# Causal masks as GpSimd selections, a division over two PSUM banks, more transposes by DMA, and chained weight loads in a one-core transformer block

## The chip, the cores and the metric

The kernel runs on one core of a Trainium2 chip. The core has five engines that run side by side, each with its own queue of instructions in order: PE (matrix products; PEld is its weight load), DVE (the vector engine), ACT (the scalar engine), POOL (GpSimd) and SP, which here issues every DMA. Engines wait for each other by semaphores. The metric is the device time of one execution in microseconds (us), smaller being better. The span of a profile runs from the first to the last instruction.

## What is computed

The reference is one transformer block over 2048 tokens of width 640, conditioned by a vector c: sliding-window attention with 32 heads of width 20, then a gated MLP of width 1536. Cut to what matters here:

```python
mod = (silu(c) @ w_mod).reshape(1, 6, 1, 640)         # sa, ca, ga, sb, cb, gb
h = layernorm(x) * (1 + ca) + sa
q, k, v = heads(h @ wqkv)                             # 32 heads, Dh = 20
scores = q @ k.T * 20 ** -0.5
mask = (i - j >= 0) & (i - j < 256)                   # i: query, j: key
p = softmax(where(mask, scores, -1e9))
x = x + ga * ((p @ v) @ wo)
h = layernorm(x) * (1 + cb) + sb
x = x + gb * ((sigmoid(h @ w_gate) * (h @ w_up)) @ w_down)
```

A query sees its own key and the 255 before it. The mask is therefore a triangle at the two ends of the window and all ones between them. The kernel applies it after the exponential, by making the forbidden weights zero.

## The kernel before

The 2048 tokens are cut into 8 chunks of 256 (numbered 0 to 7). For each chunk `ln1` loads x, takes mean and variance on DVE (L627, L629), the power -0.5 on POOL (L632, L634), normalizes (L637) and turns the result so that features lie on partitions (`hT`). For the first `NPT = 3` chunks PE turns it by products with an identity (`pe_transposes`, evicted at L670 or L671); for the others a DMA transposes it (L643) and `modulate` (L651, L652) applies scale and shift. `qkv` makes Q and K in a staging tile `stg`, head by head padded to 32 columns, and turns them into `QT` and `KT`: for the first `NPT` chunks again by identity products (evicted at L696 or L697), for the others by DMA. V stays as it comes.

`attention` works on 16 heads at a time (q = 0, 1). A **set** is a PSUM tile S of 128 x 4 x 512 scores: two groups of keys lie on its partitions 0 to 63 and 64 to 127 (called its halves), four heads in its four banks, and blocks of 64 query columns side by side. `plan` says which block stands where. Chunk 0 has four sets of 6 blocks for each q; the other chunks have five sets of 8 blocks, four of the kind "1" and one that gathers what remains, the kind "2". ACT takes the exponential of a whole set into one of 8 buffers E (L795). Then the masks: each is a TENSOR_TENSOR multiply of E by a mask tile made at the start, on DVE or POOL, as the planner chooses. The kinds are "c" (chunk 0, two of 128 x 4 x 128 a set), "d" (128 x 4 x 64) and "f" (128 x 4 x 128) on a set of kind "1" (L809), and "2" (all 2048 columns, L802) on a set of kind "2".

When the sets of a q are done, a **burst** of 128 small products (64 in chunk 0) multiplies E by V into two PSUM tiles of the pool M, in two phases of which the second waits for the first. V carries a column of ones, so the softmax's denominator comes out beside each head. `norm` then works on each of the two banks by itself: DVE transposes 32 x 32 blocks (L865), takes reciprocals (L866), multiplies (L868) and transposes back (L872). DMAs write the result to DRAM and read it back turned, `outproj` multiplies by wo and adds x (L908), the second layer norm follows, a DMA transposes, and `mlp` does gate, up and down for the chunk (L932 tanh, L934 product, L946 residual).

Nothing of this order is written out by hand. Every operation is recorded with a list of engines that may do it, a cost for each of these, a priority and what it reads and writes; score sets also have a due time (`PACE0 + PACE` times their number). A list scheduler, `Prog.schedule`, then places one operation after another on the engine where it can start first by these costs. The order on each engine is fixed when the program is built; at run time an engine takes its instructions in that order and waits where it must. SP is such an engine too: a DMA that has to wait holds back all that stand behind it. A changed cost can therefore move any instruction. `Prog.emit` adds the semaphores.

The weights (w_mod in three parts, wqkv, wo, w_gate, w_up, w_down) are loaded by 33 DMAs in the first 46 us. The second and third part of w_mod lie for a while where w_up and four of the E buffers will be, and the first where w_down will be. POOL multiplies wo and w_down by the gates ga and gb (L972 and L982).

Of the kernel before, what the change touches and what calls it, by code (L numbers as in the profile page):

```python
# [8 lines left out]
ALU = mybir.AluOpType  # L9
# [42 lines left out]
class Tile:  # L52
    __slots__ = ("pool", "name", "res", "slot", "ops", "left", "rel", "prev")

    def __init__(self, pool, name):
        self.pool = pool
        self.name = name
        self.res = {}
        self.slot = None
        self.ops = []  # L60
        self.left = 0
        self.rel = []
        self.prev = []

# [10 lines left out]
class Op:  # L75
    __slots__ = ("engs", "eng", "fn", "dur", "lat", "deps", "succ", "tiles", "prio", "seq", "nleft", "ready", "start",
                 "end", "mode", "fence", "key", "val", "signal", "work", "tmin", "isdma", "tag", "done")


class Prog:  # L80
# [8 lines left out]
    def op(self, eng, fn, dur, reads=(), writes=(), prio=50.0, lat=0.05, work=None, tmin=0.0, extra=(), tag="", hold=(),  # L89
           mode=0, fence=None):  # L90
        o = Op()
        o.mode = mode
        o.fence = fence
        o.engs = eng if isinstance(eng, tuple) else (eng,)
# [51 lines left out]
    def schedule(self):  # L146
# [27 lines left out]
        def slots_for(o):  # L174
# [4 lines left out]
            for t in o.tiles:  # L179
                if t.slot is None:  # L180
# [100 lines left out]
    def emit(self):  # L281
# [6 lines left out]
        for e in ENGS:  # L288
            for o in self.order[e]:
# [13 lines left out]
                need[o] = ws  # L303
        for e in ENGS:
# [55 lines left out]
def c_pool(n):  # L360
    return 0.22 + n / 460.0
# [7 lines left out]
NPT = 3  # L369
# [6 lines left out]
def build(nc, A_x, A_wqkv, A_wo, B_x, B_w_gate, B_w_up, B_w_down, c, w_mod, out, S=2048):  # L376
# [20 lines left out]
    mk_c = sb("mk_c", [128, 128])  # L397
    mk = sb("mk", [128, 320])
    mk_d, mk_f, mk_2 = mk[:, 0:64], mk[:, 64:192], mk[:, 192:320]
# [19 lines left out]
    p_T1 = sbpool("T1", 2, [128, 512], F32)  # L419
    p_Tn = sbpool("Tn", 2, [128, 512])  # L420
    p_On = sbpool("On", 2, [128, 1024])
    p_Dr = sbpool("Dr", 2, [128, 16], F32)
# [6 lines left out]
    p_M = Pool("M", [nc.alloc_psum_tensor(f"M{i}", [128, 512], F32) for i in range(4)])  # L429
# [9 lines left out]
    R_mA, R_shB, R_scB, R_gbc, R_mh, R_mk = R("mA"), R("shB"), R("scB"), R("gbc"), R("mh"), R("mk")  # L439

    def dma(dst, src, work, reads=(), writes=(), prio=50.0, tmin=0.0, tag="dma", extra=(), nonc=False, hold=()):
# [5 lines left out]
        return A("sp", fn, 0.43, reads=reads, writes=writes, prio=prio, work=work, tmin=tmin, tag=tag, extra=extra, hold=hold)  # L447

# [19 lines left out]
    for i in range(len(p_Tn.aps)):  # L468
        p_Tn.init[i].append(A("pool", lambda e, g, i=i: e.memset(p_Tn.aps[i][:], 0.0), 0.6, writes=[R("ti")], prio=3))

    mk_u = p_sig.aps[1][:].bitcast(BF16)[:, 0:320]

    def mk_ini(e, g):
        e.memset(mk_c[:], 1.0)
        e.memset(mk[:], 1.0)
        return e.memset(mk_u, 1.0)
    A("pool", mk_ini, 0.8, writes=[R_mk], prio=2)

    def keep(ap, w, base, cm):
        A("pool", lambda e, g: e.affine_select(ap, ap, pattern=[[-cm, w]], compare_op=ALU.is_ge, fill=0.0, base=base,  # L480
                                               channel_multiplier=cm), 0.35, reads=[R_mk], writes=[R_mk], prio=2)
    keep(mk_c[:], 128, 0, -1)
    for u in (0, 3):
        keep(mk[:, 64 * u:64 * u + 64], 64, 0, -1)
    for u in (1, 2):
        keep(mk[:, 64 * u:64 * u + 64], 64, -1, 1)
    for u in (0, 2):
        keep(mk_u[:, 64 * u:64 * u + 64], 64, 64, -1)
    for u in (1, 4):
        keep(mk_u[:, 64 * u:64 * u + 64], 64, -65, 1)  # L490
    p_sig.init[1].append(A("dve", lambda e, g: e.tensor_copy(mk[64:128, :], mk_u[64:128, :]), 0.3, reads=[R_mk], writes=[R_mk], prio=2))
# [13 lines left out]
    def load_wm(i, kt, prio, tmin=0.0):  # L505
        return dma(lambda: wm_ap[i][:, kt, :], lambda: wm_src[:, kt, i * 1280:(i + 1) * 1280], 0.86, writes=[Rm[i][kt]],
                   prio=prio, tmin=tmin, tag=f"wm{i}")
# [4 lines left out]
    def load_w3(k, prio):  # L512
        i = ("wq", "wk", "wv").index(k)
        dma(lambda: W3[k][:], lambda: wqkv_src[:, :, i * D:(i + 1) * D], 2.2, writes=[R_w3[k]], prio=prio, tag=k)
# [11 lines left out]
    dma(lambda: wo[:], lambda: A_wo.rearrange("(t p) f -> p t f", p=128), 2.2, writes=[R_wo], prio=0.5, tag="wo")  # L526
# [508 lines left out]
```

The softmax here doesn't subtract the row's maximum and nothing guards it: scores larger than these inputs give would overflow.

## Time and profile before

The times of 13 runs lie between 367.14 and 376.35 us, with a median of 371.05 us.

| | before |
|---|---|
| time of the profiled execution | 370.57 us |
| its span | 368.4 us |
| mean granted PE clock | 0.977 |
| PE busy | 337.9 us (92% of the span) |
| DVE busy | 260.9 us (71%) |
| ACT busy | 219.2 us (59%) |
| POOL busy | 139.9 us (38%) |
| masks on POOL (L802, L809) | 73 instructions, 95.8 us |
| masks on DVE (L802, L809) | 69 instructions, 41.8 us |
| products of scores and of bursts (L555) | 1920 and 1920 |
| DMA | 37.61 MB |

The span is 2.2 us shorter than the execution's time: what lies around it. A group of instructions in the profile carries its line, engine, operation, the tiles it writes and reads, its shape, its total busy time, the mean time of one, and the idle time of its engine just before it with what ended that. Products of PE overlap, so that the busy time of PE is more than the sum of its useful cycles; what counts for this kernel is when it is not busy, and when its clock is granted at half.

### The profile page before, as it was taken

What the parts mean: (1) busy time and instruction counts of PE and PEld (TensorE: products, weight loads), DVE (VectorE), ACT (ScalarE), POOL (GpSimd) and SP (SyncE); (2) the same over time, 40 slices, a digit from 0 to 9 for tenths busy, and PEclk for the clock granted to TensorE, in tenths of its full rate; (3) what the DMA queues carried; (4) which work ended last, traced back from release to release, by engine and by line L of the source; (5) the groups of instructions that cost most, each with busy time, mean ns of one, the idle gap of its engine ahead of it and who ended that gap; (6) DMA issues with size and microseconds to landing.
All of it is one profiled execution on the core that took longest, in us unless ns stands there. A gap on an engine that the chain in (4) does not pass through costs nothing.

```text
span 368.4 us, 13956 instructions
## 1 busy us (share of the span) xinstructions
PE 337.9 (92%) x6088; PEld 244.5 (66%) x6088; DVE 260.9 (71%) x543; ACT 219.2 (59%) x237; POOL 139.9 (38%) x160
## 2 busy tenths in 40 slices
PE   6898866989899899999999989899899999999996
PEld 2665433656566576667675667677767868888784
DVE  5369997999769996865857699678668866432232
ACT  1395783777688877888687667566676711122120
POOL 6127695682454632452354526255232300100000
PEclk9899995999899999999999999999999999999999
DMA  6999932206742736293015411131041122010101
GB/s 201 382 396 392 372 93 63 72 4 115 144 112 63 153 79 123 61 146 94 21 45 97 106 41 31 44 107 35 5 112 39 34 74 76 20 55 1 37 1 37
DMA packets 65181, 37.61 MB, mean 102 GB/s; under 512 B 41440, under 2 KB 61920, under 8 KB 65120
## 3 DMA queue, kind: packets, MB, share of 16 engines
q1 hardware_dynamic: 65120, 36.72, 36.7%
q8 instruction: 48, 0.79, 0.9%
q14 instruction: 13, 0.11, 0.1%
HBM read 21.96 MB, written 5.24 MB: 74 GB/s over the span
## 4 chain that ended last, share of the span: by engine, by line
PE 67%; DVE 8%; issue 3%; ACT 2%; POOL 0%; DVEq 0%; ACTq 0%
PE M L554 56%; PE M L555 6%; PE S L555 5%; DVE T L865 1%; DVE x L637 1%; ACT E L795 1%; DVE st L627 1%; DVE x L908 1%; DVE Tn L868 1%; DVE hT L652 1%; DVE On L872 1%; DVE E L809 1%; ACT sig L932 0%; DVE stg L697 0%; DVE h2T L652 0%
## 5 line engine op out<-in xcount | busy, mean ns | idle before, releaser
L795 ACT ACTIVATE E<-S 128x2048 bf16<-128x2048 f32 (+1 forms) x78 | 142.9, 1833 | 46.8 <-PE S L555 46.1
L809 POOL TENSOR_TENSOR E<-E,mk 128x256 bf16<-128x256 bf16 (+1 forms) x59 | 55.0, 943 | 96.0 <-ACT E L795 91.5
L554 PE MATMUL M<-h2T,wg 128*128 128x256 bf16 x480 | 64.1, 275 | 1.5 <-ACT h2T L651 0.8
L554 PE MATMUL M<-h2T,wu 128*128 128x256 bf16 x480 | 64.3, 276 | 1.0 <-DVE x L946 0.7
L554 PE MATMUL M<-wd,hh 128*128 128x320 bf16 x384 | 55.7, 299 | 1.6 <-DVE hh L934 0.7
L932 ACT ACTIVATE sig<-M 128x512 f32<-128x512 f32 x48 | 28.6, 596 | 47.9 <-PE M L554 43.3
L934 DVE SCALAR_TENSOR_TENSOR hh<-sig,M 128x512 bf16<-128x512 f32 x48 | 32.6, 682 | 34.1 <-PE M L554 32.2
L554 PEld LDWEIGHTS M<-h2T,wg 128*128 128x128 bf16 x480 | 45.8, 98 | 9.7 <-issue 0.9
L554 PEld LDWEIGHTS M<-h2T,wu 128*128 128x128 bf16 x480 | 46.0, 99 | 8.9 <-DVE x L946 1.0
L554 PEld LDWEIGHTS M<-wd,hh 128*128 128x128 bf16 x384 | 36.6, 98 | 16.8 <-DVE hh L934 1.2
L802 POOL TENSOR_TENSOR E<-E,mk 128x2048 bf16<-128x2048 bf16 x8 | 32.5, 4062 | 13.2 <-ACT E L795 13.1
L555 PE MATMUL S<-QT,KT 20*64 20x128 bf16 (+3 forms) x1920 | 33.6, 238 | 2.8 <-ACT E L795 1.9
L555 PEld LDWEIGHTS S<-QT,KT 20*64 20x64 bf16 x1920 | 19.4, 104 | 21.7 <-issue 11.8
L946 DVE TENSOR_TENSOR x<-M,x 128x320 bf16<-128x320 f32 x32 | 15.6, 489 | 21.9 <-PE M L554 21.5
L555 PE MATMUL M<-E,V 64*32 64x128 bf16 (+3 forms) x1920 | 25.4, 234 | 6.1 <-issue 1.5
L865 DVE STREAM_TRANSPOSE T<-M 128x512 f32<-128x512 f32 x32 | 21.0, 693 | 12.1 <-PE M L555 12.1
L555 PEld LDWEIGHTS M<-E,V 64*32 64x32 bf16 x1920 | 20.6, 90 | 12.4 <-issue 5.6
L627 DVE BATCH_NORM_STATS2 st<-x 128x6 f32<-128x320 bf16 x64 | 28.2, 471 | 0.6 <-DMA x<-in_A_x_dram 0.4
L554 PE MATMUL M<-wq,hT 128*128 128x320 bf16 x160 | 27.3, 310 | 1.4 <-DVE scB L979 1.1
L809 DVE TENSOR_TENSOR E<-E,mk 128x512 bf16<-128x512 bf16 (+1 forms) x53 | 24.1, 471 | 5.9 <-ACT E L795 5.3
L554 PE MATMUL M<-wk,hT 128*128 128x320 bf16 x160 | 26.4, 306 | 1.9 <-DVE QT L697 1.3
L637 DVE TENSOR_SCALAR x<-x,st 128x640 bf16<-128x640 bf16 x32 | 25.2, 814 | 4.0 <-POOL st L634 4.0
(77 smaller groups left out, 398.5 us busy)
## 6 DMA issues: line engine op xcount, KB each, us to landing
x<-in_A_x_dram SPq DMA_DIRECT2D x32, 160.0 KB, 6.3
doc<-On SPq DMA_DIRECT2D x64, 40.0 KB
out_dram<-x SPq DMA_DIRECT2D x16, 160.0 KB
wg<-in_B_w_gate_dram SPq DMA_DIRECT2D x5, 384.0 KB
wd<-in_B_w_down_dram SPq DMA_DIRECT2D x4, 480.0 KB
wu<-in_B_w_up_dram SPq DMA_DIRECT2D x5, 384.0 KB
wd<-in_w_mod_dram SPq DMA_DIRECT2D x5, 320.0 KB
wu<-in_w_mod_dram SPq DMA_DIRECT2D x5, 320.0 KB
```

The lines of the kernel that those rows point to most:

```text
L554: return e.matmul(o, l, r, start=st, stop=sp, skip_group_check=True)
L555: return e.matmul(o, l, r, start=st, stop=sp, tile_position=tp, skip_group_check=True)
L627: A("dve", lambda e, g, bi=bi, j=j: e.bn_stats(v(bi * 12 + j * 6, 6), src[bi].ap[:, j * 320:(j + 1) * 320]), 0.48, reads=[src[bi].r()], wr ...
L637: A("dve", lambda e, g, bi=bi: e.tensor_scalar(dst[bi].ap[:], src[bi].ap[:], v(24 + 2 * bi, 1), v(30 + bi, 1), op0=ALU.subtract, op1=ALU.m ...
L652: return e.tensor_scalar(ap, ap, sc[:, dt:dt + 1], sh[:, dt:dt + 1], op0=ALU.mult, op1=ALU.add)
L795: A("act", lambda e, eng: e.activation(E.ap[:, :, 0:W], Sp.ap[:, :, 0:W], ACT.Exp, scale=SM_SCALE), c_act(4 * W), reads=[Sp.r()], writes=[ ...
L802: return e.tensor_tensor(ap, ap, mk_2.unsqueeze(1).to_broadcast([128, 16, 128]), op=ALU.mult)
L809: return e.tensor_tensor(ap, ap, t.unsqueeze(1).to_broadcast([128, 4, w]), op=ALU.mult)
L865: A("dve", lambda e, g: e.transpose(T1.ap[:], O.ap[:]), 0.714, reads=[O.r()], writes=[T1.r()], prio=3.5, tag="tr1")
L932: A("act", lambda e, g, pg=pg, sg=sg: e.activation(sg.ap[:], pg.ap[:], ACT.Tanh, scale=0.5), c_act(512), reads=[pg.r()], writes=[sg.r()], ...
L934: A("dve", lambda e, g, pu=pu, sg=sg, f0=f0: e.scalar_tensor_tensor(out=hh.ap[:, f0:f0 + 2, :], in0=sg.ap[:].rearrange("p (a b) -> p a b", ...
L946: A("dve", lambda e, g, ps=ps, bi=bi, half=half: e.tensor_tensor(x1[bi].ap[:, half * 320:half * 320 + 320], ps.ap[:, 0:320], x1[bi].ap[:, ...
```

## The change

Six things are changed.

- **Masks.** The mask tiles are gone. A mask is now made by `affine_select` on POOL alone: it keeps E where an affine function of partition and column is not negative, and writes zero elsewhere, in place. The blocks of a set of kind "1" are put in a new order so that the triangles of one half lie at regular distances. Such a set takes four selections: on partitions 0 to 63 one of 4 x 64 and one of 8 x 64 columns, and on 64 to 127 one of 8 x 64 and one of 4 x 64. A set of kind "2" takes two of 16 x 64, one on each half. Chunk 0 takes two of 128 x 4 x 128 a set. Where two POOL operations that follow each other work on different partitions, the second now waits for the first (`part`).
- **Pieces.** The new order cuts the scores of a half into four pieces instead of three: 2368 products for the scores instead of 1920, and as many for the bursts, on the same number of columns.
- **Division on two banks.** The two M tiles of a burst must now be neighbours (`mate`). After two transposes of 128 x 512, `norm` does one reciprocal, one multiply and one transpose back of 128 x 1024 for both.
- **Transposes.** PE turns hT for chunks 0 and 1 only (`NPH = 2`), and Q and K for chunk 0 only (`NPQ = 1`). DMA does the rest: 14 instead of 10 transposes each for QT and KT, and 12 instead of 10 for hT.
- **Chained loads.** Each large weight load now also waits for the landing of the sixth before it (`DEEP = 6`).
- **Costs.** The planner's costs are changed for selections on POOL, for modulation and for evictions.

By the order that the planner makes of it, PE has 32 identity products on `stg` instead of 96 and 20 on x instead of 30. DVE has no masks, 1 eviction of QT or KT instead of 11, 36 of stg instead of 26, 15 of V instead of 11, and 40 modulations instead of 35. The 12 multiplications of w_down now stand on POOL ahead of most masks of chunk 1, 7 of them in a row.

```diff
+        for p, o in zip(self.order["pool"], self.order["pool"][1:]):
+            if p.part != o.part and p not in need[o]:
+                need[o].append(p)
+                p.signal = True
...
 def c_pool(n):
-    return 0.22 + n / 460.0
+    return 0.22 + n / 1150.0
...
-NPT = 3
+NPH = 2
+NPQ = 1
+DEEP = 6
...
+    def chain():
+        return [bulk[-DEEP]] if len(bulk) >= DEEP else []
...
-            A(("dve", "act"), mo, {"dve": 0.33, "act": 0.43}, reads=...
+            A(("dve", "act"), mo, {"dve": 0.4, "act": 0.59}, reads=...
...
-        if a < NPT:
+        if a < NPH:
             pe_transposes(src, t, scA, shA, [R_mA], 1)
...
-                if a < NPT:
+                if a < NPQ:
...
-            sets.append(([(k, 0, 0, 4, 0), (k, -1, 0, 3, 4), (k, -2, 0, 1, 7)],
-                         [(b, 0, 1, 3, 0), (b, -1, 0, 4, 3), (b, 1, 3, 1, 7)], 8, ((0, "d"), (6, "f"))))
+            sets.append(([(k, -1, 0, 3, 0), (k, 0, 0, 3, 3), (k, -2, 0, 1, 6), (k, 0, 3, 1, 7)],
+                         [(b, 0, 1, 3, 0), (b, -1, 0, 1, 3), (b, 1, 3, 1, 4), (b, -1, 1, 3, 5)], 8, "1"))
...
-                def mk(e, eng, t=t, w=w, cu=cu):
-                    ap = E.ap[:, :, cu * 64:cu * 64 + w]
-                    return e.tensor_tensor(ap, ap, t.unsqueeze(1).to_broadcast([128, 4, w]), op=ALU.mult)
-                dur = {"dve": c_dve(4 * w, 2.0), "pool": c_pool(4 * w)}
-            A(("dve", "pool"), mk, dur, reads=[E.r(), R_mk], writes=[E.r(cu)], prio=5, tag=f"mask{a}")
...
+        def keep_d(e, ap):
+            return e.affine_select(ap, ap, pattern=[[0, ap.shape[1]], [1, ap.shape[2]]], compare_op=ALU.is_ge, fill=0.0,
+                                   base=0, channel_multiplier=-1)
...
+        elif mks == "1":
+            mask([lambda e: keep_d(e, col(0, 3, 8)), lambda e: keep_f(e, col(0, 2, 4))], [256, 512], 0, 0)
+            mask([lambda e: keep_d(e, col(64, 0, 4)), lambda e: keep_f(e, col(64, 7, 8))], [256, 512], 1, 1)
+        else:
+            mask([lambda e: keep_d(e, col(0, 0, 2))], [1024], 0, 0)
+            mask([lambda e: keep_f(e, col(64, 1, 2))], [1024], 1, 1)
...
         X = [Tile(p_M, f"O{a}_{q}x"), Tile(p_M, f"O{a}_{q}y")]
+        X[0].mate, X[1].mate = X[1], X[0]
...
+        A("dve", lambda e, g: e.reciprocal(Dr.ap[:], T1.ap[:, DH:1024:32]), 0.35, reads=[T1.r(0), T1.r(1)], writes=[Dr.r()],
...
+        A("dve", lambda e, g: e.tensor_tensor(blk(Tn), blk(T1), Dr.ap[:].unsqueeze(2).to_broadcast([128, 32, DH]), op=ALU.mult),
+          0.83, reads=[T1.r(0), T1.r(1), Dr.r()], writes=[Tn.r()], prio=4, tag="divide")
+        A("dve", lambda e, g: e.transpose(On.ap[:], Tn.ap[:]), 1.22, reads=[Tn.r()], writes=[On.r()], prio=4, tag="tr2")
```

## The prediction

> **What bounds the kernel now.** I read the page first: the busy shares, and the chain of work that ended last by engine.
>
> ```profile
> span 368.4 us, 13956 instructions
> ...
> PE 337.9 (92%) x6088; PEld 244.5 (66%) x6088; DVE 260.9 (71%) x543; ACT 219.2 (59%) x237; POOL 139.9 (38%) x160
> ...
> PE 67%; DVE 8%; issue 3%; ACT 2%; POOL 0%; DVEq 0%; ACTq 0%
> ```
>
> The chain runs through PE, so the end moves by three things: PE's own work, the time PE idles, and the time its clock is at half. Next the busy time by stretches (columns: us, busy of PE, PEld, DVE, ACT, POOL with their instructions, granted clock, DMA share, GB/s).
>
> ```profile
> 33.00:47.00 14.00, 11.19 (x208) 6.74 (x205) 13.59 (x26) 9.57 (x13) 10.88 (x9) 1.00 0.96 354
> 47.00:53.40 6.40, 4.88 (x156) 2.85 (x154) 6.40 (x15) 5.51 (x7) 5.67 (x7) 1.00 0.36 94
> 53.40:58.10 4.70, 0.01 (x4) 0.00 (x0) 4.70 (x5) 1.88 (x1) 4.47 (x4) 0.71 0.17 44
> 58.10:66.00 7.90, 7.63 (x62) 4.51 (x63) 5.41 (x14) 3.32 (x4) 4.35 (x5) 0.53 0.24 68
> 66.00:100.00 34.00, 30.50 (x659) 20.22 (x656) 32.20 (x74) 25.99 (x31) 18.99 (x18) 0.95 0.45 86
> 100.00:200.00 100.00, 95.38 (x2095) 67.13 (x2095) 75.42 (x168) 79.90 (x85) 44.34 (x40) 1.00 0.46 92
> 200.00:300.00 100.00, 94.95 (x2061) 70.52 (x2058) 76.49 (x152) 63.53 (x52) 37.08 (x33) 1.00 0.21 55
> 300.00:368.40 68.40, 65.01 (x548) 53.51 (x548) 26.81 (x52) 13.45 (x23) 0.93 (x2) 1.00 0.12 35
> ```
>
> From 33 to 58 us DVE is busy 24.7 of 25.1 us: there it is the bound, and PE idles 2.8 + 1.5 + 4.7 = 9.0 us. Behind the last hole the clock is 0.53 for 7.9 us, which costs another 7.9 x 0.47 = 3.7 us. After 66 us PE idles 3.5 + 4.6 + 5.1 + 3.4 = 16.6 us in all, in many small gaps.
>
> Why DVE is full there, the groups by shape and one line's range (min/median/max) say:
>
> ```profile
> L802 POOL TENSOR_TENSOR E<-E,mk 128x2048 bf16<-128x2048 bf16 x8 | 32.5, 4062 | 13.2 <-ACT E L795 13.1
> L809 POOL TENSOR_TENSOR E<-E,mk 128x512 bf16<-128x512 bf16 x26 | 31.2, 1199 | 17.2 <-ACT E L795 17.2
> ...
> L809 POOL TENSOR_TENSOR E<-E,mk 128x256 bf16<-128x256 bf16 x33 | 24.5, 741 | 78.8 <-ACT E L795 74.3 <-issue 2.5 <-DVE On L872 2.0
> ...
> L480 POOL TENSOR_SCALAR_AFFINE_SELECT sig<-sig 128x64 bf16<-128x64 bf16 x4 | 1.0, 241 | 0.3
> ...
> L480 POOL TENSOR_SCALAR_AFFINE_SELECT mk_c<-mk_c 128x128 bf16<-128x128 bf16 x1 | 0.3, 295 | 0.0
> ```
>
> ```profile
> L637 DVE TENSOR_SCALAR x<-x,st x32: 425/441/4328, 8.1 to 314.9; 128x640 bf16<-128x640 bf16 x32
> ```
>
> The same instruction takes 0.44 or 4.33 us. The long cases began under a POOL multiply and ended with it (at 225 us a mask of 4.06 us). DVE's masks and modulations (L652, 0.34 to 4.0 us) are held likewise; its block transposes are not (0.67 to 0.72). Two multiplies in a row held it only until the first ended (at 55.35 us: 1.51 us, the first over after 1.33). Short POOL work holds for short: at 8.10 us, beside selections of 0.24 and a memset of 0.53, two L637 took 1.16 instead of 0.88.
>
> **The change, part by part.**
>
> *PE's work.* 64 identity products on stg go. Four of them end 0.22 us before the next product may start (17.80 to 18.02 us): 16 x 0.22 = 3.5 us. Ten on x go, about 1.0 us. The 448 extra score products cost nearly nothing: a set of 24 occupies PE for 0.35 us (182.03 to 182.38), one of 32 on the same columns for 0.36 (84.52 to 84.88); 56 x 0.01 = 0.6 us. The 448 extra ones of the bursts lie between 0, if columns set the pace, and 14 x 1.73 x 32/128 = 6.1 us, if each costs what one of 128 in 1.73 us does. The nearest row is the score set, which goes by columns; I take 1 us. Net -4.5 + 1.6 = **-2.9 us**, bounds -4.5 to +2.2.
>
> *Masks.* DVE loses 69 multiplies, 41.8 us, and its evictions, modulations and casts change by about -8.5 (QT, KT and hT) + 8.5 (stg, V, hT). So DVE falls from 261 to some 219 us, less what the shorter holds give back. POOL loses 95.8 us and must carry everything. A selection's price: 241 ns for 64 columns and 295 for 128, so 0.84 ns a column; 256 columns make 0.40 us, 512 0.61 and 1024 1.04. A q of chunks 1 to 7 takes 4 x 2 x (0.40 + 0.61) + 2 x 1.04 = 10.2 us. The new waits on POOL cost little, by the four selections that stood chained at 9.43 us (1.17 us for 0.97 of work, so 0.07 a wait): 0.7 us a q. That is 10.9 us, where bursts now come every 17.9 us (47 to 297 us, 14 of them). Behind the waiting selection stand only masks and the layer norm's small operations, for which DVE waits up to 1 us more. The upper bound is the multiply's rows: 4 x 2 x (0.74 + 1.20) + 2 x 2.1 = 19.7 us a q. It stands far from the selections' own rows, and I take 10.9. Nothing of it lies on the path while POOL keeps ahead of the bursts; if not, the second rival's price is due. At the start POOL has 16 selections for chunk 0 (9.8 us), 12 of its 17 multiplications of wo and w_down (1.44 each, 17.3 us) and three layer norms (2.8 us) ahead of chunk 1's masks, from 26 us on: to 56 us, when the first exponential of chunk 1 ends too. ACT loses about 10 us of evictions and is no bound.
>
> The Trainium skill's GPSIMD Engine Reference, section Engine selection, advises against GpSimd for elementwise work (about half of VectorE's speed with two inputs) but puts one input near line rate. Its best case in Elementwise — side-by-side cycle accounting, 768 ns for 512 elements, would make 12.3 us a q instead of 10.2.
>
> *The hole at 33 to 66 us* (9.0 + 3.7 us). DVE sheds 11.8 us of masks before 60 us (ten of L809 on mk_c, 9.6 us, and 2.2 at 53.25), the casts of chunk 1's QT and KT, and waits under POOL's multiplications. It now normalizes chunk 2, for which PE waited 4.7 us, before it evicts the projections of chunk 1. What is late next: Q and K of chunk 1 come by DMA, from the end of an SP queue in which the weight loads stand before them, each waiting for the sixth before it. The loads filled the DMA queue until about 45.5 us. SP issues a transpose in 1.2 to 1.3 us. Two hT and three QT or KT now stand among the loads. At 89 to 95 us three QT or KT, the tail of an h2T and small transfers kept the queue 0.96 busy, so one is below 1.9 us; I take 1.5, and 6 for all five. The last KT can then land at 45.5 + 6 + 2.7 (its issue to landing) = 54 us. By the order, PE has between the last w_mod product (33.0 us before) and the first score set of chunk 1 110 projections at 0.136 (five in 0.68 at 22.82 us), four score sets at 0.30 and two bursts (1.1 and 1.5): 18.8 us. So it gets there at 52, against 47 before, with chunk 2's projections nearly done, and waits 2 us. With 2.7 us for other waits 8 of the 12.7 us are gained: **-8 us**, bounds -12 (no wait) and +2 (KT 10 us late, with a half clock again).
>
> On transposes the Trainium skill speaks against the change: VectorE: DVE Perf Modes, section The three transpose paths, lists 1309 ns by DMA against 390 on TensorE for 128 x 128. At that price eight blocks in a row would take 10.5 us and the last KT would come after 80 us. The trace's 2.7 us to landing decides.
>
> *The rest.* The last set of a burst waited for a mask of 4.06 us (8 times, POOL) or 1.22 (6 times, DVE), on average 2.8; now for 2.1 on POOL. The holds of DVE shrink from up to 4 us to at most about 1. The division saves the fixed part of three instructions a burst, off the path, and I count it as nothing: the small gaps of MLP products hide it, and without them it would be under 0.5 us a burst. The pair of neighbouring banks can only delay a burst, by an eviction of 0.7 us at most. Of 16.6 us of gaps I take **-2 us**, bounds -8 and +10.
>
> Sum: 368.4 - 2.9 - 8 - 2 = 355.5 us of span, and 2.2 around it: 357.7. The profiled execution (370.57) stands at the median shown (371.05), so I forecast **357.5 us**. Within 1% of 371.05 is about what a measurement of this kernel cannot tell from no change.
>
> **The rivals.**
>
> 1. *The hole only moves.* PE waits for KT of chunk 1 or hT of chunk 2 behind the weight loads, the clock drops again, and DVE's relief goes into its new casts. For: KT and POOL are both ready only as PE arrives. Against: chunks 2 and 3 are there to project meanwhile. Time: 370.6 - 2.9 + 0 to 2 = 368 to 370.
> 2. *POOL becomes the bound.* Selections in this form (three dimensions, 64 partitions) cost what the multiplies cost: 19.7 us a q. From 54 us, 14 q at 19.7 and 12 us of layer norms end at 342. Behind the last mask stand a division (3.6), the trip through DRAM (5), the output projection (2.7), LN and transposes (7) and one MLP (120 x 0.109 + 48 x 0.136 = 19.6): 38 us. End 380 + 2 = 382, so 377 to 392. It decides from 18 us a q on ((355.5 - 38 - 54 - 12) / 14), that is when 512 columns cost over 1.0 us. For: only one selection of 128 columns and none with three dimensions is in the trace. Against: the slope of those there are.
> 3. *It does not do what it says:* selections hold DVE as long in sum as multiplies did, since they come more often. Then DVE still drops by 41.8 us of masks, and only the -2 goes: 359 to 361, inside the forecast's range.
>
> **Chances.** Forecast with the third rival 0.66 (347 to 366); first rival 0.15; second 0.14; other slips of the newly planned order, slower, 0.05. The range runs from 346 to 379: it holds the first two cases, the first part of the second rival and both ends of the bounds but the farthest. Faster 0.66, same 0.15, slower 0.19.
>
> **What would show it.** Selections of 8 x 64 near 0.6 us and POOL near 200 us busy; no L637 over 1.6 us; DVE below 225 us; PE busy through 50 to 60 us with the clock at 1.00 there; first scores of chunk 1 near 54 us; bursts of 160 products under 1.9 us. Wrong if selections of 512 columns take over 1.0 us, if PE waits for KT or hT beyond 57 us, or if PE's gaps after 66 us exceed 20 us.

## The result, and the profile after

The changed kernel is slower: 384.83 us, median of 11 runs (379.93 to 392.49), against 369.22 us for the kernel before on the same chips. The ratio is 1.038, with an interval of 1.035 to 1.042. It compares the faster executions of the two kernels (382.8 and 368.7 us on average), since each also has some that are about 2% slower, and the profiled executions of the changed kernel and of three runs below (no chain; numbers + 182; Q and K by DMA) are among those. Forecast were 357.5 us and a range that ended at 379. The profiled execution took 385.87 us, with a span of 384.1 us, 15.7 us more than before.

The page of the changed kernel, the lines that answer to those of before; PEclk is the granted PE clock in 40 slices, and q8 is the DMA queue that brings instructions (packets, MB, share):

```profile
span 384.1 us, 15727 instructions
PE 344.0 (90%) x6910; PEld 249.8 (65%) x6910; DVE 218.0 (57%) x431; ACT 210.1 (55%) x215; POOL 203.9 (53%) x342
PEclk9999978967999999989999998998989999999999
...
q8 instruction: 54, 0.88, 1.0%
...
PE 72%; issue 7%; DMA 6%; POOL 6%; ACT 5%; DVE 2%; SPq 1%; POOLq 0%; DVEq 0%; ACTq 0%
```

DVE and POOL came out as forecast (below 225 and near 200). PE is busy 6 us longer, and the share of "issue" in the chain, time in which an engine waits for nothing that the profile names, rose from 3 to 7%. The mean granted clock fell from 0.977 to 0.960. By stretches, with the columns of before:

```profile
33.00:47.00 14.00, 12.33 (x142) 7.09 (x126) 7.18 (x15) 9.93 (x14) 11.42 (x14) 1.00 1.05 288
47.00:53.40 6.40, 3.73 (x141) 2.19 (x139) 4.38 (x7) 1.36 (x4) 4.44 (x4) 0.99 1.11 354
53.40:58.10 4.70, 3.58 (x14) 2.10 (x15) 4.63 (x6) 0.88 (x2) 4.70 (x4) 0.50 1.43 153
58.10:66.00 7.90, 5.22 (x119) 3.19 (x118) 3.40 (x7) 5.66 (x6) 4.90 (x9) 0.87 0.90 213
66.00:100.00 34.00, 28.22 (x760) 17.99 (x759) 23.75 (x55) 23.54 (x19) 27.74 (x46) 0.85 0.71 125
100.00:200.00 100.00, 91.10 (x2379) 66.38 (x2380) 65.31 (x127) 70.15 (x68) 72.65 (x118) 0.98 0.49 83
200.00:300.00 100.00, 92.16 (x2199) 67.97 (x2184) 55.52 (x102) 60.12 (x49) 58.66 (x100) 0.95 0.22 54
300.00:384.10 84.10, 79.39 (x872) 64.98 (x869) 34.87 (x65) 21.58 (x31) 7.31 (x12) 1.00 0.15 37
```

DVE is no longer full at 33 to 53 us (11.6 of 20.4 us), but PE still idles 8.1 us of the 33 us up to 66 (9.3 before). After 66 us it idles 5.8 + 8.9 + 7.8 + 4.7 = 27.2 us instead of 16.6; the prediction had named 20 as the limit.

What PE waited for in the changed kernel (us in total, times, longest), the first rows:

```profile
PE M L564 <- issue: 8.0, 6, 1.8
PE S L564 <- issue: 6.8, 5, 2.0
PE S L564 <- ACT E L803: 6.5, 6, 2.1
PE M L563 <- issue: 5.4, 2, 3.5
PE M L563 <- DVE stg L706: 2.0, 2, 1.7
```

Three of the five rows say "issue": 13 stops, 20.2 us. Before there were 4 of over 0.35 us, 2.7 us in all. The selections and their waits are not among the causes: PE waited 0.6 us for POOL in all. (The chain has 6% on POOL, mostly selections that a burst needed, as at 67.4 to 75.8 and 132.3 to 143.6 us; PE had other products for nearly all of that time.) This was one of the 13, in PE's timeline of the changed kernel (start, duration, what, and in brackets the idle time before it):

```profile
112.25 1.92 PE L564 MATMUL M<-E,V 64*32 64x192 bf16 x160
114.10 0.39 PE L563 MATMUL M<-h2T,wg 128*128 128x256 bf16 x2
116.35 0.39 PE L563 MATMUL M<-h2T,wg 128*128 128x256 bf16 x2 [1.86 <-issue]
116.68 0.43 PE L564 MATMUL S<-QT,KT 20*64 20x192 bf16 x32
```

A burst ends, two MLP products run, and then PE stands for 1.86 us between two products of the same kind, before one for which no semaphore wait is recorded.

**The pattern.** A product is two PE instructions, a weight load and a multiplication. Count them in the trace in order of start, with the semaphore and drain instructions of PE's queue. The stop above lies before instruction 3777 = 14 x 256 + 193. All 13 stops lie at 193 over a multiple of 256. The queue q8 brought 54 packets of 16 KB for 13,915 such instructions, one for each 256; before, 48 for 12,264. In each of the 13 stops, work goes on 1.3 to 1.6 us after the end of such a packet. So PE had run out of instructions. From the 140th instruction of one page to the 193rd of the next are 309. In the 18 profiles listed below, the n-th packet never began earlier than 0.9 us after the 140th instruction of the n-th page, and after 66 us those 309 never took less than 3.4 us, with a stop or without. A burst of 320 instructions lasts 1.7 us. (Some expectations below take 4.2 us for the 309.)

The Trainium skill tells of this in Runtime: NRT & Kernel Launch, section Instruction fetch mechanics: instructions are fetched in blocks of 16 KiB, 256 instructions, the next while the current one runs, and the fetch is said to be hidden because instructions are issued slower than they come. The 256 agrees with the packets here; that it is hidden does not hold where PE takes 320 instructions in 1.7 us.

### The profile page after: what moved, and what is told of

It is laid out like the page before. It is cut to its first block, busy times and chain, and to the rows that moved or that the text cites. A ratio compares the mean times of both kernels' runs of the same rounds, so it can differ in the third digit from the quotient of the medians.

```text
span 384.1 us, 15727 instructions
## 1 busy us (share of the span) xinstructions
PE 344.0 (90%) x6910; PEld 249.8 (65%) x6910; DVE 218.0 (57%) x431; ACT 210.1 (55%) x215; POOL 203.9 (53%) x342
## 4 chain that ended last, share of the span: by engine, by line
PE 72%; issue 7%; DMA 6%; POOL 6%; ACT 5%; DVE 2%; SPq 1%; POOLq 0%; DVEq 0%; ACTq 0%
PE M L563 58%; PE M L564 8%; PE S L564 7%; ACT E L803 5%; DMA hT<-x 2%; DMA x<-in_A_x_dram 2%; POOL E L808 2%; POOL E L812 2%; DMA wd<-in_w_mod_dram 2%; POOL wd L1007 1%; SPq L465 1%; DVE hT L661 0%; PE S L563 0%; POOL st L643 0%; DVE st L636 0%
## 5 line engine op out<-in xcount | busy, mean ns | idle before, releaser
L808 POOL TENSOR_SCALAR_AFFINE_SELECT E<-E 64x256 bf16<-64x256 bf16 (+3 forms) x142 | 89.1, 630 | 81.6 <-ACT E L803 73.6
L812 POOL TENSOR_SCALAR_AFFINE_SELECT E<-E 64x512 bf16<-64x512 bf16 (+2 forms) x126 | 76.8, 609 | 1.0
L563 PE MATMUL M<-h2T,wg 128*128 128x256 bf16 x480 | 65.6, 278 | 1.9 <-issue 1.9
L564 PE MATMUL S<-QT,KT 20*64 20x192 bf16 (+3 forms) x2368 | 35.9, 229 | 13.3 <-issue 6.8
L564 PEld LDWEIGHTS S<-QT,KT 20*64 20x64 bf16 x2368 | 23.8, 108 | 33.3 <-issue 17.2
L564 PE MATMUL M<-E,V 64*32 64x64 bf16 (+3 forms) x2368 | 29.5, 222 | 10.9 <-issue 8.0
L564 PEld LDWEIGHTS M<-E,V 64*32 64x32 bf16 x2368 | 23.8, 90 | 17.9 <-issue 9.9
L563 PE MATMUL M<-wk,hT 128*128 128x320 bf16 x160 | 28.0, 315 | 5.2 <-issue 3.5
L971 DVE TENSOR_TENSOR x<-M,x 128x320 bf16<-128x320 f32 x32 | 15.7, 490 | 27.7 <-PE M L563 27.7
L563 PE MATMUL M<-wo,oT 128*128 128x320 bf16 x160 | 27.2, 319 | 0.0
L563 PE MATMUL M<-wv,hT 128*128 128x320 bf16 x160 | 25.8, 309 | 0.0
## 6 DMA issues: line engine op xcount, KB each, us to landing
wg<-in_B_w_gate_dram SPq DMA_DIRECT2D x5, 384.0 KB
wu<-in_B_w_up_dram SPq DMA_DIRECT2D x5, 384.0 KB
```

The costliest lines, as they stand in the source:

```text
L563: return e.matmul(o, l, r, start=st, stop=sp, skip_group_check=True)
L564: return e.matmul(o, l, r, start=st, stop=sp, tile_position=tp, skip_group_check=True)
L808: return e.affine_select(ap, ap, pattern=[[0, ap.shape[1]], [1, ap.shape[2]]], compare_op=ALU.is_ge, fill=0.0, base=0, channel_multiplier=-1)
L812: return e.affine_select(ap, ap, pattern=[[0, ap.shape[1]], [-1, ap.shape[2]]], compare_op=ALU.is_ge, fill=0.0, base=-1, channel_multiplier=1)
L971: A("dve", lambda e, g, ps=ps, bi=bi, half=half: e.tensor_tensor(x1[bi].ap[:, half * 320:half * 320 + 320], ps.ap[:, 0:320], x1[bi].ap[:, ...
```

## The experiments

The theory after this reading (F): PE can't take more than some 300 instructions in 4 us, the bursts do, and so the extra pieces cost more than their columns or their own time. The rivals: waits on POOL or the order planned around it; the transposes by DMA; the chained loads. "Stalls" below are stops of PE, of 0.35 us and more and without a semaphore, at instruction 193 over a multiple of 256, in number and us, of the profiled execution.

| kernel | time / before (interval) | span us | stalls |
|---|---|---|---|
| before | 1 | 368.4 | 3, 2.3 |
| changed | 1.038 (1.035 to 1.042) | 384.1 | 13, 20.2 |
| before, pieces split | 1.055 (1.038 to 1.072) | 391.1 | 11, 14.9 |
| before, numbers + 154 | 1.007 (1.003 to 1.012) | 371.8 | 4, 3.7 |
| before, gate products split | - | 369.3 | 4, 4.0 |
| before, order nudged | 1.016 (1.011 to 1.021) | 371.5 | 3, 4.3 |
| changed, three pieces | 1.029 (1.017 to 1.040) | 376.1 | 6, 10.1 |
| changed, PE transposes | 1.036 (1.027 to 1.045) | 380.4 | 11, 18.9 |
| changed, no chain | 1.042 (1.022 to 1.061) | 386.6 | 12, 16.6 |
| changed, numbers + 70 | 1.071 (1.059 to 1.083) | 394.9 | 12, 22.5 |
| changed, numbers + 182 | 1.032 (1.021 to 1.044) | 386.0 | 10, 15.1 |
| **both**: three pieces and PE transposes | 0.973 (0.964 to 0.982) | 358.4 | 4, 4.6 |
| both, but Q and K by DMA | 0.999 (0.994 to 1.003) | 368.8 | 7, 9.2 |
| both, but hT of chunk 2 by DMA | 0.991 (0.988 to 0.995) | 360.1 | 5, 8.5 |
| both, no chain | 1.005 (1.001 to 1.009) | 368.0 | 4, 4.5 |
| both, old division | 0.996 (0.992 to 1.000) | 365.8 | 6, 7.9 |
| both, no chain, old division | 1.016 (1.009 to 1.022) | 370.0 | 1, 2.0 |
| both, order nudged | 0.994 (0.990 to 0.998) | 365.8 | 5, 5.4 |

In these 18 profiles there are 118 stops of PE of 0.5 us and more that no semaphore explains; 114 stand at exactly 193. The span grows by 1.3 us for each us of stalls (a line through the 18 points, correlation 0.82).

### The pieces alone, added to the kernel before

```diff
-            sets.append(([(k, 0, 0, 4, 0), (k, -1, 0, 3, 4), (k, -2, 0, 1, 7)],
-                         [(b, 0, 1, 3, 0), (b, -1, 0, 4, 3), (b, 1, 3, 1, 7)], 8, ((0, "d"), (6, "f"))))
+            sets.append(([(k, 0, 0, 3, 0), (k, 0, 3, 1, 3), (k, -1, 0, 3, 4), (k, -2, 0, 1, 7)],
+                         [(b, 0, 1, 3, 0), (b, -1, 0, 1, 3), (b, -1, 1, 3, 4), (b, 1, 3, 1, 7)], 8, ((0, "d"), (6, "f"))))
```

> The kernel before with nothing changed but the pieces: the block of 4 x 64 query columns that one product takes is given in two (3 and 1), so that there are 2368 products for the scores and as many for the bursts, on the same columns at the same places, and the order of all other instructions is that of before. Theory F (PE runs out of instructions): the bursts carry 320 instructions in about 1.85 us instead of 256 in 1.66, stalls without a semaphore appear at 449 over a multiple of 256 executed instructions, some 10 to 20 us in sum, and the time grows by 8 to 18 us, to 377 to 387 us. Rival W (products cost their own small time, nothing else): 14 bursts x 0.19 us + 56 sets x 0.01 us, +3 us, 371 to 374 us, with stalls without semaphore as before, 2.7 us.

It took 5.5% more (392.2 us), with a span 22.7 us longer: the 14.9 us of stalls are what theory F had, the time is above the ranges of both theories. PE's waits in this kernel:

```profile
PE M L555 <- issue: 9.4, 7, 1.9
PE S L555 <- issue: 5.9, 5, 2.1
PE M L554 <- DVE KT L697: 4.9, 1, 4.9
PE M L554 <- DVE x L637: 4.8, 1, 4.8
PE M L554 <- issue: 2.4, 1, 2.4
```

"issue" is 17.7 us here, 15.0 more than before. A burst that no stall hits lasts 1.66 us from its first to its last start, instead of 1.51: 14 x 0.15 = 2.1 us, and the score sets 0.5. That is 17.6 of the 22.7 us; the lower clock (391.1 x 0.026 us lost, for 368.4 x 0.023) takes 1.7, and a new wait for an eviction of KT at 66.7 us is the largest of the rest. The rival, 3 us, falls. This is the clean test: on every engine the order of all other work is that of before, also in the trace.

### The pieces undone, the transposes undone, the chain undone

```diff
-            sets.append(([(k, -1, 0, 3, 0), (k, 0, 0, 3, 3), (k, -2, 0, 1, 6), (k, 0, 3, 1, 7)],
-                         [(b, 0, 1, 3, 0), (b, -1, 0, 1, 3), (b, 1, 3, 1, 4), (b, -1, 1, 3, 5)], 8, "1"))
+            sets.append(([(k, 0, 0, 4, 0), (k, -1, 0, 3, 4), (k, -2, 0, 1, 7)],
+                         [(b, 0, 1, 3, 0), (b, -1, 0, 4, 3), (b, 1, 3, 1, 7)], 8, "1"))
...
-            mask([lambda e: keep_d(e, col(0, 3, 8)), lambda e: keep_f(e, col(0, 2, 4))], [256, 512], 0, 0)
+            mask([lambda e: keep_d(e, col(0, 0, 8)), lambda e: keep_f(e, col(0, 6, 8)), lambda e: keep_f(e, col(0, 7, 8))],
+                 [256, 256, 256], 0, 0)
```

> The changed kernel, but with the old order of blocks: three pieces a half, so 1920 products for the scores and 1920 for the bursts instead of 2368 each, on the same columns; a set of kind "1" then takes six selections of 4 x 64 instead of two of 4 x 64 and two of 8 x 64, and the planner reorders the rest a little. Theory F (PE runs out of instructions): in the profile of the changed kernel PE stands 20 us in stalls that no semaphore explains, before 2.7 us, each where the number of executed instructions is 449 over a multiple of 256, and the stalls are followed by half clock. With 1792 instructions fewer, the bursts are again 256 in 1.66 us, as before: the stalls fall to under 5 us, the half clock outside the start to under 10 us, and the time to 358 to 368 us. Rival P (the selections and their waits on POOL, or the order planned around them, delay the bursts): the stalls have little weight, POOL's six selections a set cost slightly more (6 x 0.43 instead of 2 x 0.43 + 2 x 0.66), and the time stays at 380 to 388 us.

Neither theory hit: half of the stalls went (10.1 us are left, not under 5), but the time, 380.4 us, was the rival's. So the pieces are not the whole cause. From 60 to 100 us this kernel's PE waits were these:

```profile
PE S L564 <- ACT E L803: 7.9, 6, 2.1
PE M L564 <- issue: 1.6, 1, 1.6
```

```profile
33.00:66.00 33.00, 26.31 (x403) 15.30 (x400) 20.04 (x36) 18.75 (x25) 27.24 (x35) 0.90 1.10 265
66.00:100.00 34.00, 26.39 (x577) 15.59 (x582) 22.52 (x51) 22.79 (x19) 27.81 (x62) 0.75 0.66 130
```

Where two score sets follow each other in PE's order, the second waits 2 us for the exponential that frees its S (three times, and three shorter waits), and the clock is 0.75. PE's order has nothing else at these places.

```diff
-NPH = 2
-NPQ = 1
+NPH = 3
+NPQ = 3
```

> The changed kernel with the transposes by identity products of the kernel before (hT, Q and K of chunks 0 to 2 on PE). Theory F (PE runs out of instructions): the stalls without a semaphore stay, 15 to 25 us in sum, since the bursts are the same; only those of the first 60 us may move; 378 to 392 us. Rival D (the transposes by DMA, which stand among the weight loads and delay both Q and K of chunk 1 and the instruction pages): the time falls to 366 to 374 us, and the stalls outside the first 66 us become few.

381.9 us and 18.9 us of stalls, as F said. PE is busy 29.9 of the 33 us up to 66, at full clock, 6 us more than before: what was forecast for the hole at the start does come, if the transposes stay on PE. The stalls, 16.6 us more than before, are more than that.

```diff
-DEEP = 6
+DEEP = 99
```

> The changed kernel without the chain of the weight loads: each large load is issued without waiting for the sixth before it. Theory F (PE runs out of instructions): the stalls after 66 us stay at 14 to 20 us in sum, as they come from the bursts; the time stays within 4 us of the changed kernel's, 380 to 390 us. Rival D (the loads' chain places the transposes among the loads, and the start is what costs the time): the time moves by more than 6 us, and the stalls after 66 us fall below 8 us.

387.4 us, 16.6 us of stalls after 66 us: with four pieces and transposes by DMA, no difference that the chain makes can be told (1.042 with its interval, for 1.038).

### The same kernels with other instruction numbers

The warm-up's products are cut, so that all later instructions get a higher number and the page limits fall elsewhere in the same work.

```diff
-            ins = e.matmul(p_S.aps[0][:, 0, :], Eall[:, 0, 0:128], Eall[:, 0, 128:640], start=True, stop=True)
+            n = 64 if 2 * i + k < 5 else 512
+            for c in range(0, 512, n):
+                ins = e.matmul(p_S.aps[0][:, 0, c:c + n], Eall[:, 0, 0:128], Eall[:, 0, 128 + c:128 + c + n], start=True,
+                               stop=True)
```

> The changed kernel with 5 of its 18 warm-up products cut into 8 each, so that every later PE instruction has a number 70 higher; nothing else. Theory F: by the same two figures (asked for at 140, 4.2 us) the stalls without a semaphore after 60 us grow from 15.6 us worked out (16.7 measured) to 23 us, 12 or 13 of them, most of 2.1 to 2.5 us; the time is 5 to 9 us above the changed kernel's 384.8, so 389 to 395 us. Rival W: within 1.5 us of the changed kernel.

> The changed kernel with 13 of its 18 warm-up products cut into 8 each, so that every later PE instruction has a number 182 higher; nothing else. Theory F: the stalls after 60 us fall from 15.6 us worked out (16.7 measured) to 8 us, near 108, 111, 142, 177, 227, 286 and 304 us; the time is 6 to 12 us below the changed kernel's 384.8, so 373 to 379 us, and 12 to 20 us below the run shifted by 70. Rival W: within 1.5 us of the changed kernel.

> The kernel before, instruction for instruction, except that 11 of the 18 warm-up products of 512 columns at the start are cut into 8 of 64 columns each: the same columns, 77 products more, so every later PE instruction has a number 154 higher. Theory F (PE's instructions come in pages of 256; the page is asked for near instruction 140 of the one before, and instruction 193 of the next page cannot run until about 4.2 us later): shifting the numbers moves the page limits within the bursts. Worked out from the trace of before with these two figures, the stalls grow from 1 us (2.7 measured) to 7 us, at new places, near 78, 180, 200, 222, 268 and 288 us, and each at 193 over a multiple of 256; the time grows by 4 to 8 us, to 374 to 379 us. Rival W (products and waits alone count): nothing after the warm-up changes, within 1.5 us of before.

The first came nearly as worked out: 22.5 us of stalls for 23, and 396.6 us, a little above the 389 to 395. PE's waits there (the lines of this kernel lie 3 lower):

```profile
PE M L567 <- issue: 13.5, 7, 2.3
PE S L567 <- issue: 9.0, 5, 2.5
```

The second did not: 15.1 us of stalls instead of 8, and 384.0 us, no better than the changed kernel. The third went the right way, but by 0.7% and not 1 to 2, with 3.7 us of stalls for 7. (A stop of 1.7 us at 78.0 us, where before has none, is not counted: it lies at 193 and ends 1.4 us after a packet, but the profile puts it down to an exponential.) So a page limit's place counts (the same order of work differs by 12.6 us between the first and the second), every stop of 0.5 us and more without a semaphore in these three runs again stands at 193, and the two figures (140 and 4.2 us) tell where it is worst but not how good it gets: a stall removed moves the work behind it, which then meets its own limits.

### As many instructions, where PE is slow

```diff
+                    if tag.startswith("mlpg"):
+                        mm(e, o[:, 0:128], l, r[:, 0:128], k == 0, False)
+                        ins = mm(e, o[:, 128:256], l, r[:, 128:256], False, k == len(pairs) - 1)
+                        continue
```

> The kernel before, but every product of the gate (h2T times w_gate, 256 columns) is given in two of 128 columns: 480 products more, 960 instructions, about as many as the split pieces added (896 products), but in the MLP, where PE takes an instruction every 0.055 us and not every 0.006. The order of everything else is that of before. Theory F in its full form (what counts is how many instructions come within some 4.2 us, not how many there are): no stalls in the MLP; those of the bursts only change with the place of the page limits, 1 to 8 us in sum; the products themselves add 0 to 5 us; 371 to 380 us. Rival N (every page fetched costs time wherever it lies): stalls in proportion to the instructions, 10 us and more, as with the split pieces; 382 us and more.

The profiled execution took 371.44 us, its span 0.9 us more than that of before, with 4.0 us of stalls, each of which begins less than 1.7 us behind the end of a burst and none in a stretch of MLP products alone. (Its four runs took 371.4, 372.3, 378.5 and 381.1 us; no ratio is given. The first two are some 1% above before.) With 960 instructions more, at most some 1%, and no stalls where they were added: what counts is how many come at once, not how many there are.

### Pieces and transposes both undone

The edits of the runs with three pieces and with PE transposes, together.

> The changed kernel with both the old three pieces a half (1920 and 1920 products) and the old transposes on PE (hT, Q and K of chunks 0 to 2); selections on POOL, the division on two banks and the chained loads stay. In the two runs with one of these undone, the old transposes kept PE busy for 29.9 of the 33 us from 33 to 66 us at full clock (23.7 in the kernel before), and the old pieces brought the stalls without a semaphore down to 10 us. Theory F: together, stalls of 1 to 7 us, depending on where the page limits fall, and the gain of the freed DVE is left: 358 to 368 us, faster than both kernels. Rival P (masks on POOL alone cost the time in waits of the bursts): 374 to 382 us, as in the run with three pieces alone.

360.8 us, as F said, 2.7% faster than before (0.973, 0.964 to 0.982) and 6% faster than the changed kernel. POOL's six selections a set are those of the run with three pieces alone, so they were not what held that one up. Each undoing by itself won 1% or less of the time of before, both together 6.5%: either fault alone is enough to lose the time. The stretches:

```profile
33.00:66.00 33.00, 29.89 (x557) 18.85 (x555) 26.11 (x52) 25.41 (x31) 29.35 (x47) 1.00 0.69 217
66.00:100.00 34.00, 31.40 (x681) 21.54 (x679) 25.77 (x56) 25.46 (x27) 29.26 (x61) 0.95 0.72 114
100.00:200.00 100.00, 90.31 (x1983) 63.38 (x1981) 66.22 (x127) 64.52 (x59) 76.70 (x155) 1.00 0.42 76
```

To 100 us PE works 7.1 us more than before; from 100 to 200 us it works 5.1 us less. Its waits there, for evictions between MLPs that follow each other directly:

```profile
PE M L563 <- DVE hh L961: 2.7, 3, 1.0
PE M L563 <- DVE x L935: 2.1, 4, 0.7
PE M L564 <- issue: 1.5, 1, 1.5
PE M L563 <- ACT sig L959: 1.4, 2, 0.7
```

So most of what is won at the start is given back later.

### Which transposes, and what the other parts are worth

```diff
-NPQ = 3
+NPQ = 1
```

> The version with three pieces and all old transposes (360.8 us), but Q and K of chunks 1 and 2 turned by DMA as in the changed kernel; hT of chunks 0 to 2 stays on PE. With both kinds by DMA three pieces took 380.4 us, so the two kinds together cost some 19 us there. Theory Q (Q and K of chunk 1 come by DMA from a queue that the weight loads fill, the instruction page that PE needs near 50 us stands behind the same load, and PE then has no other work ready): most of the 19 us is here, 374 to 382 us, PE busy under 28 us from 33 to 66 us, and a stall of over 2 us near 50 us at 193 over a multiple of 256. Rival H (hT of chunk 2 by DMA is what comes late): 360 to 366 us here.

```diff
-NPH = 3
+NPH = 2
```

> The version with three pieces and all old transposes (360.8 us), but hT of chunk 2 turned by DMA as in the changed kernel; Q and K of chunks 0 to 2 stay on PE. Theory Q (Q and K by DMA are what costs): 360 to 367 us, PE busy over 28 us from 33 to 66 us. Rival H (hT of chunk 2): 374 to 382 us.

368.6 and 365.0 us. By the ratios, these two kinds cost 0.026 and 0.018 of the time of before, where both together cost 0.056 (1.029 with three pieces alone, 0.973 here). In the first run theory Q saw the stall near 50 us (2.4 us, at 193) and PE at 27.3 us up to 66, but not the time. The second run's time is in its range, but that run has such a stall too (4.1 us), without much harm. Neither kind is the cause alone.

```diff
-DEEP = 6
+DEEP = 99
...
-        norm(X, On)
+        for h in range(2):
+            norm(X[h], On, h)
```

> The version with three pieces and the old transposes (360.8 us), with the old division on each bank by itself and without the chain of the weight loads: against the kernel before only the masks, as selections on POOL, and the planner's costs are changed. Theory M (the freed DVE is the whole gain; division and chain are worth nothing): 358 to 365 us, PE busy over 29 us from 33 to 66 us. Rival C (the chain or the joint division carries the gain): 366 to 371 us.

373.2 us, 1.6% slower than before: both theories wrong. To find out what lay between, the two parts were undone singly, and the planner was nudged without any change of work:

```diff
-PACE0 = 15.0
+PACE0 = 15.3
```

> The version with three pieces and the old transposes (360.8 us) without the chain of the weight loads; the division on two banks stays. Without both chain and joint division it took 373.2 us. Theory C (the chain carries the 12 us): 370 to 375 us. Rival V (the joint division carries them): 359 to 363 us. Rival O (neither; it is the order that the planner happens to make, which every edit changes): somewhere between, and then the same edit-free nudge of the planner moves the time by some 4 us and more too.

> The version with three pieces and the old transposes (360.8 us) with the old division on each bank by itself; the chain of the weight loads stays. Theory V (the joint division carries the 12 us that lie between 360.8 and 373.2): 370 to 375 us. Rival C (the chain carries them): 359 to 364 us. Rival O (the order that the planner happens to make): somewhere between.

> The version with three pieces and the old transposes (360.8 us), with nothing changed but the due time of the first score set in the planner, 15.3 instead of 15.0 us: the same instructions in another order. Theory O (the order that the planner happens to make is worth several us): 364 to 372 us. Otherwise within 3 us of 360.8.

> The kernel before with nothing changed but the due time of the first score set in the planner, 15.3 instead of 15.0 us: the same instructions in another order. Theory O (the order that the planner happens to make is worth several us, and the order of before is a good one): 373 to 382 us, with more stalls at 193 over a multiple of 256 than the 2.7 us of before. Otherwise within 3 us of the kernel before.

The chain undone: 370.0 us, at the edge of what theory C gave; the division undone: 367.6 us, in between, as rival O had it; the order nudged: 367.3 us, and the kernel before, nudged: 374.1 us, both as theory O said. The nudge alone moves one kernel by 2.1% and the other by 1.6%, as much as either part. So the order that the planner happens to make is worth some 2%, the 360.8 us are partly luck, and what chain and division are worth by themselves can't be told from these runs. The five versions with the selections, three pieces and PE transposes lie between 0.973 and 1.016 of before, on average 0.997: the masks on POOL, for which the rest was done, win nothing that stands above this. In all five PE was busy 28.1 to 30.0 us of the 33 up to 66 (23.7 before), and 88.3 to 91.6 us from 100 to 200 (95.4 before): won, and given back. What stands above it are the pieces (5.5%, with the order unchanged) and the two kinds of transposes together (0.056 of the time of before, or some 20 us, with three pieces).

## Why the prediction was wrong

**PE's work: the step that failed.** "The 448 extra ones of the bursts lie between 0, if columns set the pace, and 14 x 1.73 x 32/128 = 6.1 us ... I take 1 us." Their own time was 2.5 us in the changed kernel (14 bursts of 1.69 us from first to last start, for 1.51), inside the bounds. But the pieces cost 22.7 us of span where they alone were changed, because both bounds were prices of a product and neither asked where the instructions come from. Three rows in the profile of before pointed there: q8 with one packet for each 256 instructions; "issue" with 3% of the chain; and stops of 0.5 to 1.0 us at 145.8, 233.4 and 262.3 us, at 193 over a multiple of 256, with no semaphore behind them. They were not followed up. The first row, and what PE waited for under "issue" after 60 us, in the profile of before:

```profile
q8 instruction: 48, 0.79, 0.9%
```

```profile
PE M L555 <- issue: 1.4, 2, 0.9
PE S L555 <- issue: 1.0, 2, 0.8
PE M L554 <- issue: 0.5, 1, 0.5
```

Dividing would have done: 320 instructions in 1.7 us use up a page of 256 in 1.4 us, while at these three stops of before the next page's packet took 1.25 to 1.35 us and work went on 1.25 to 1.70 us after its end.

**The clock behind the stalls.** Stops that the sum did not have also cost clock. Busy time and granted clock around one of them, in the changed kernel:

```profile
160.00:162.60 2.60, 2.53 (x172) 1.81 (x169) 0.36 (x2) 0.77 (x2) 2.07 (x5) 1.00 1.23 120
162.60:164.40 1.80, 0.01 (x1) 0.00 (x0) 1.10 (x2) 0.00 (x0) 0.03 (x1) 1.00 0.52 109
164.40:165.90 1.50, 1.46 (x32) 1.10 (x33) 0.29 (x1) 0.98 (x1) 0.00 (x0) 1.00 0.91 182
165.90:169.40 3.50, 3.50 (x45) 1.95 (x44) 3.18 (x6) 2.71 (x5) 2.46 (x4) 0.51 1.41 102
```

After 1.8 us without work come 3.5 us at half clock, 1.7 us lost. Four of the 13 stalls were followed so (162.6, 234.5, 259.9, 275.3 us), others of the same length were not. The clock's own record tells them apart. Its changes lie on a grid of 3.41 us, and the four stops left PE busy for 0.43 to 0.50 of one slot of that grid; the stops that began at 114.5 and 312.5 us, 1.8 to 1.9 us long, are split by a line of the grid and left 0.53. In the 18 profiles, after 50 us, 47 of the 57 full-clock slots with PE busy under 0.53 were followed by a slot at half, and no slot with more than 0.59 was. Over the span the clock cost 384.1 x 0.040 = 15.4 us, against 368.4 x 0.023 = 8.5 before.

**The hole: the mechanism right, the transfers mis-sized.** PE no longer waits 4.7 us for x, as said. But "the last KT can then land at 45.5 + 6 + 2.7 = 54 us" failed: the first score of chunk 1 came at 59.7 us, where 54 was forecast and 47.2 measured before. In the changed kernel SP took 2.1 to 2.7 us for each of the three transposes that it issued from 46 to 54 us, not 1.2 to 1.3, and the DMA engines were full to 53.9 us and again from 55.2 to 57. In the run with the numbers moved by 70, where no page came late at 50 us, PE's chain shows what it waited for instead (start, us, what):

```profile
47.97 1.46 PE M L566 x11
49.43 8.30 DMA KT<-stg
57.74 0.04 issue
57.78 0.27 PE S L567
```

8.3 us from issue to landing instead of 2.7. In the changed kernel itself PE stood 3.5 us at 51 us for an instruction page whose packet began only at 52.2 us, under the same load. The first score of chunk 1 followed there on projections without a wait, at half clock from 53.3 us, so a late KT is shown for the other run alone, and for the changed kernel the late page and the clock. Of the forecast -8 us, 1.2 us of idle time remained, and from 66 to 100 us PE idled 2.3 us more than before, at a clock of 0.85 instead of 0.95. The first rival had named this ("PE waits for KT of chunk 1 ... behind the weight loads, the clock drops again") and got 0.15.

**The rest.** -2 us became +10.6 us of idle time after 66 us: the stalls there are 16.7 us, for 2.3 before, and the other waits did become shorter.

As a sum, the changed kernel against before: stalls and other "issue" +17.5, clock +6.9, the extra products +3, transposes on PE -4.5 (the forecast's figure, not measured by itself), other stops of over 0.35 us -5.6 (19.3 before, 13.7 after), in all +17.3, for 15.7 measured.

**What was right.** The price of the selections and what DVE sheds. The selections' groups by shape, and L646 (min/median/max):

```profile
L808 POOL TENSOR_SCALAR_AFFINE_SELECT E<-E 64x512 bf16<-64x512 bf16 x56 | 36.9, 658 | 3.9
L812 POOL TENSOR_SCALAR_AFFINE_SELECT E<-E 64x256 bf16<-64x256 bf16 x56 | 24.1, 430 | 0.0
L812 POOL TENSOR_SCALAR_AFFINE_SELECT E<-E 64x1024 bf16<-64x1024 bf16 x14 | 16.0, 1145 | 1.0
```

```profile
L646 DVE TENSOR_SCALAR x<-x,st x32: 342/447/1421, 8.0 to 332.7; 128x640 bf16<-128x640 bf16 x32
```

0.66, 0.43 to 0.47 and 1.14 us, where 0.61, 0.40 and 1.04 were taken; no hold of 4 us is left. With that the second rival falls: PE waited 0.6 us for POOL. The third falls in part: L646 took 19.6 us in all, for 25.2 before, but DVE's modulations took 0.59 us (h2T) and 0.49 (hT) on average, for 0.57 and 0.54, so those were held about as before. Right prices made no right sum, since the time was lost elsewhere.

**Open.** What a page's 1.4 us from its packet to the next instruction consist of, and why four of the 118 stops lie elsewhere, was not found. How the cost of the transposes divides between late pages, late KT and the order planned around them is not settled either; and no version was made that keeps four pieces and spreads the bursts.

## What to carry to other kernels

Price a burst of small products also by its instructions: on this chip PE's instructions came in pages of 256, and where its order would take more than about 300 within less than some 4 us, PE stood up to 2.5 us at the page limit, and up to 4.1 where the DMA engines were full, with nothing but "issue" to show for it. Count instructions in the trace at such stops. More and smaller pieces are cheap among large products and dear in a burst. And where a planner makes the order, nudge it without changing the work before crediting an edit with 2%.

## What was not expected of the hardware

- The stops lie at one instruction number: 114 of 118 at 193 over a multiple of 256. Work goes on 1.1 to 1.7 us (median 1.4) after the end of the packet, which itself takes 0.9 to 1.6 us.
- Instruction pages came late when the DMA engines were full of data: a packet of the changed kernel began 7.0 us after instruction 140 of the page before, where it was 1 to 5 us after 66 us, and PE stood 3.5 us.
- Stops of 1.7 to 2.0 us were enough, four times of 13, for 3.4 us at half clock: those that left PE busy for at most half of one slot of 3.41 us. The Trainium skill (TensorE: Matmul & The Clock Gate, section HAM oscillation — how this bites in real kernels) names idle gaps above 3.4 us; these traces show the loss at half of that.
